# Threshold attention and a gated feed-forward block on one core: a smaller first part of the first batch, and its first block of tokens in two units

## The chip, the core and the metric

The kernel runs on one core of a Trainium2 chip. A core has five engines that run side by side, each with its own instruction stream in program order: TensorE (PE, matrix products into PSUM), VectorE (DVE), ScalarE (ACT), GpSimd (POOL) and SyncE (SP, which here issues the loads). They wait for each other through semaphores. The metric is the device time of one execution in microseconds (us), the median of several runs.

## The reference

```python
scores = scale * np.matmul(q, k.transpose(0, 1, 3, 2))        # (8 batches, 8 heads, 576, 576), head size 64
thresh = np.max(scores, axis=-1, keepdims=True) - tau
scores = np.where(scores >= thresh, scores, -1000000000.0)
scores = scores - np.max(scores, axis=-1, keepdims=True)
attn = np.exp(scores)
attn = attn / (np.sum(attn, axis=-1, keepdims=True) + 1e-09)
y = np.matmul(attn, v)
x = y.transpose(0, 2, 1, 3).reshape(4608, 512)                # tokens x model width
g = x @ w_gate                                                # 512 -> 1536
out = g * (1.0 / (1.0 + np.exp(-g))) * (x @ w_val) @ w_out    # 1536 -> 512
```

The three weight matrices arrive as 64-bit floats and are turned into 32-bit ones on the chip. All matrix products are in 32 bits; PE runs each as two instructions.

## The kernel before, in words

**Attention.** Heads are taken in pairs, four pairs to a batch, 32 in all. A *step* is one query tile of one pair: tiles 0 to 3 have 128 queries, tile 4 has 64. In a step PE makes the scores (L254 to L264), DVE takes their maximum (L274, L284), ACT makes the exponentials (L290), DVE applies the threshold and sums (L294), takes the reciprocal (L302), and ACT or POOL scales the rows (L308, L306). A full tile's scores fill both score buffers, so the next step's scores wait for this step's L294.

**Batch 0 is different.** Its four pairs are run in two parts: first tiles 0, 1 and 2 of each pair (`early`, `TA = 3` tiles, 384 queries), then tiles 3 and 4 of each (`rest`). So the first 384 tokens are complete for all heads before the rest is begun. In batch 0 PE turns the probabilities (L338) and multiplies by v (L361) within the next two steps. From batch 1 on (`halved`) all five tiles of a pair run in a row, DVE turns the probabilities (L320), and the product with v is made once per pair (L389), in the second step of the next pair. `prepare` (L591) puts a pair's q and k through DVE transposes at the end of the last step but one of the pair before; in batch 0 the queries that the first part does not use are kept in a spare arena.

**The feed-forward block** works on chunks of 384 tokens (`TC`), as *units* (chunk, first token, end). Chunk 1 is in two units of 192, since batch 0 ends in its middle; the others are whole. A unit runs through 12 slices `f` of the hidden width: `gate` (L423: four matmuls, then ACT copies the result to a `gt` tile, L434) and `value` (L436: four matmuls, then DVE multiplies with `gt` into `ht`, L442). Every second `f` an entry goes on the list `unsig`; when it holds three (`SIG`), `sigmoids` (L449) turns all entries: ACT makes the sigmoid of `gt` in place, with a table load before it and another when the next exponential comes, and POOL multiplies it into `ht` (L452). Only then is a `gt` tile free: there are four (`gp`, L76), each for two slices. `output` (L458) then makes rows of 128 tokens, in pieces of three slices (L466).

**PSUM.** Gates, values, outputs, turned probabilities and attention products take turns in four buffers (`ps_f`, L80).

**Weights.** They come in 24 pieces. Per step `fetch_weights` issues loads into free places on SP, `split_weights` lets ACT take one piece apart (L155, L156), and `join_weights` rebuilds it: four operations on DVE (L168 to L174) and two on POOL (L176, L177). The last pieces use only two places, so their split comes straight after their load. `need` forces joins when a slice lacks its weights.

**The order.** It is written out by the loop at the end (L633 on). Per step: scores; attention product or turning of earlier tiles; `fetch_weights` and `split_weights`; threshold and sum; join; half a share of feed-forward work (`fill`); scaling; `sigmoids` if three entries wait; the other half share; then loads and `prepare`. The share comes from `pace` (L570): the units left are spread over the steps until the next units are due, at the lowest rate over all horizons. `cost` counts a unit: one for each matmul of 384 tokens, four for each output piece. Units become ready (`give`) when their tokens are complete: the first at the start of the second part of batch 0.

Of the kernel before, what the change touches and what calls it, by code (L numbers as in the profile page):

```python
# [18 lines left out]
def kernel(  # L19
# [26 lines left out]
    nc = tc.nc  # L46
    P = 128
    B, H, S, D = q.shape
# [13 lines left out]
    TC = 384  # L62
    NCHUNK = B * S // TC
    NPAIR = B * NP
    TA = TC // P
    SCALE = 1.0 / float(D) ** 0.5
    assert 2 * D == P and NCC == NP and D == 2 * G and S - SM == 2 * G and 2 * S % TC == 0

# [349 lines left out]

    unsig = []

    def gate(j, cs, f, hts, gts):  # L423
# [56 lines left out]
    ready = deque()  # L480
    waiting = deque()
    for j in range(NCHUNK):
        if j == 1:
            waiting.extend([(1, 0, S - TC), (1, S - TC, TC)])
        else:
            waiting.append((j, 0, TC))

    def rows_of(unit):
        j, lo, hi = unit
        return range(lo // P, hi // P)  # L490

    def cost(unit):
        return 2 * NF * HCOST * (unit[2] - unit[1]) / TC + len(rows_of(unit)) * NF / OF * OCOST

    def supply(done):

        got = []
        while waiting and waiting[0][0] * TC + waiting[0][2] <= done:
            got.append(waiting.popleft())
        return got  # L500
# [3 lines left out]
    def block():  # L504
        late = iter(())
        while True:
            if not ready:
                yield from late
                if not ready:
                    yield 0  # L510
                continue
            unit = ready.popleft()
            j, lo, hi = unit
            cs = slice(lo, hi)
            hts, gts = hidden.setdefault(j, {}), {}
            c = HCOST * (hi - lo) / TC
            for f in range(NF):
                if f == (EARLY if j else 0):
                    yield from late
                gate(j, cs, f, hts, gts)  # L520
                yield c
                value(j, cs, f, hts, gts)
                yield c
            late = output(j, rows_of(unit), hts)
# [25 lines left out]
    arenas = [ptp.tile([P, 2 * NT + 1, S], F32, name="p") for _ in range(2)]  # L550
    early = list(range(TA))
    rest = list(range(TA, NT + 1))
    flat = [x.rearrange("p n s -> p (n s)") for x in arenas]
# [7 lines left out]
    for n, seg in enumerate(segs):  # L561
        done = 0
        if n == NP - 1:
            done = TC
        elif n % NP == NP - 1:
            done = n // NP * S
        seg["gives"] = supply(done)
        gains.append((len(seg["tiles"]), sum(cost(u) for u in seg["gives"])))
# [16 lines left out]
    kept = {}  # L585
# [5 lines left out]
    def prepare(seg):  # L591

        i = seg["i"]
        if i in kept:
            seg.update(kept[i])
            return
        qr, kr = raws[i]
        kept[i] = None
        qT = qkp.tile([P, S], F32, name="qT")
        if i < NP:  # L600
            kT = arenas[0][:, 4 + i, :]
            rest = flat[0][:, i * (S - TC):(i + 1) * (S - TC)]
            nc.vector.transpose(out=kT, in_=kr)
            nc.vector.transpose(out=qT[:, 0:TC], in_=qr[:, 0:TC])
            nc.vector.transpose(out=rest, in_=qr[:, TC:S])
            kept[i] = {"kT": kT, "qT": rest, "q0": TC}
        else:
            kT = qkp.tile([P, S], F32, name="kT")
            nc.vector.transpose(out=kT, in_=kr)
            nc.vector.transpose(out=qT, in_=qr)  # L610
        seg.update(kT=kT, qT=qT, q0=0)
# [6 lines left out]

    fetch_qk(0)
    prepare(segs[0])  # L620
    fetch_weights(1)
    fetch_qk(1)
# [4 lines left out]
    for n, seg in enumerate(segs):  # L627
        if NP <= n < 2 * NP:
            seg["v"] = segs[seg["i"]]["v"]
        for x, t in enumerate(seg["tiles"]):  # L630
# [37 lines left out]
            if x == len(seg["tiles"]) - 2 and n + 1 < len(segs):  # L668
                prepare(segs[n + 1])
                fetch_qk(segs[n + 1]["i"] + 1)  # L670
# [40 lines left out]
```

## Time and profile before

| | |
|---|---|
| median of 3 runs | 1619.55 us (1617.14 to 1622.19) |
| profiled execution | 1617.98 us, of which span 1616.2 us, mean granted PE clock 0.986 |
| busy PE, DVE, POOL, ACT | 1547.4, 1082.5, 771.3, 583.5 us |
| gate and value matmuls of 384 tokens | 1056 instructions each |
| gate and value matmuls of 192 tokens | 192 instructions each |
| first gate matmul | at 96.2 us |
| step 20, the first of batch 1, its L294 | at 167.59 us |
| ACT table loads | 23 before sigmoids, 22 before exponentials, 1.283 us each |

The span runs from the first to the last instruction. Busy times of PE are modelled, and overlapping matmuls are counted once. In lines of the profile, L433 is a line of the kernel, `pg<-xT,wgv` says what is written from what, x8 is a count, and the bracket at the end of a row says how long the engine sat idle before it and what ended that. In a group's row, "37.6, 340" are the busy time in us and the mean of one instruction in ns.

### The profile page before, as it was taken

The numbers are of one execution on the slowest core, as the hardware profiler recorded it, in microseconds if no ns is written. First come the engines' busy times: TensorE is split into PE (matmuls) and PEld (weight loads), VectorE is DVE, ScalarE is ACT, GpSimd is POOL, SyncE is SP. The second block draws the span as 40 slices with busy tenths as digits, with TensorE's granted clock in tenths as the row PEclk, the third lists the DMA queues.
The fourth block names the chain that finished last, engine by engine and source line by source line (L and its number), as shares of the span: only waits on it lengthen the run. The fifth ranks groups of instructions, "written<-read, shape, count | busy, mean of one in ns | idle before, by whom it ended". The sixth has DMA issues, their size and how long they took to land.

```text
span 1616.2 us, 27669 instructions
## 1 busy us (share of the span) xinstructions
PE 1547.4 (96%) x10192; PEld 831.2 (51%) x10192; DVE 1082.5 (67%) x3660; ACT 583.5 (36%) x1302; POOL 771.3 (48%) x686
## 2 busy tenths in 40 slices
PE   6899779899999999999999999999999999999998
PEld 4555444557545455455545545455545545455453
DVE  6977978876888778777766768677767767501000
ACT  6867543333324323323323424323323424312011
POOL 3545365555555645646545555645445554402011
PEclk9999889999999999999999999999999999999999
DMA  6542221111111111111011111111011110000000
GB/s 166 152 138 63 66 50 37 44 37 31 30 43 31 46 35 30 44 37 28 6 43 36 30 50 30 44 37 19 12 44 37 30 50 16 8 13 1 13 7 19
DMA packets 176343, 66.68 MB, mean 41 GB/s; under 512 B 159568, under 2 KB 159568, under 8 KB 176208
## 3 DMA queue, kind: packets, MB, share of 16 engines
q1 hardware_dynamic: 173328, 55.47, 15.1%
q0 software_dynamic: 2880, 9.44, 1.5%
q8 instruction: 81, 1.33, 0.3%
q14 instruction: 54, 0.44, 0.1%
HBM read 55.44 MB, written 9.44 MB: 40 GB/s over the span
## 4 chain that ended last, share of the span: by engine, by line
PE 77%; DVE 13%; ACT 4%; issue 3%; POOL 1%; DMA 1%; SPq 1%; DVEq 0%; POOLq 0%; ACTq 0%
PE pg L433 20%; PE pv L441 20%; PE po L466 19%; PE sc L254 8%; PE xa L389 8%; DVE p L294 3%; DVE mx L274 2%; DVE p L320 1%; ACT p L290 1%; DVE mx L231 1%; POOL p L306 1%; ACT L290 1%; SPq L203 1%; DVE sums L231 1%; POOL ht L452 0%
## 5 line engine op out<-in xcount | busy, mean ns | idle before, releaser
L306 POOL TENSOR_SCALAR p<-p,ri 128x288 f32<-128x288 f32 x486 | 479.0, 1001 | 439.2 <-DVE ri L302 435.1
L433 PE MATMUL pg<-xT,wgv 128*128 128x384 f32 (+1 forms) x1248 | 405.8, 469 | 6.0 <-ACT gt L434 4.0
L441 PE MATMUL pv<-xT,wgv 128*128 128x384 f32 (+1 forms) x1248 | 406.3, 469 | 0.0
L466 PE MATMUL po<-wo,ht 128*128 128x512 f32 x864 | 386.4, 599 | 1.2 <-POOL ht L452 1.2
L433 PEld LDWEIGHTS pg<-xT,wgv 128*128 128x128 f32 x1248 | 230.0, 191 | 159.2 <-issue 21.9
L441 PEld LDWEIGHTS pv<-xT,wgv 128*128 128x128 f32 x1248 | 231.5, 192 | 152.7 <-issue 17.8
L294 DVE SCALAR_TENSOR_TENSOR p<-sc,th,p 128x288 f32<-128x288 f32 (+1 forms) x540 | 258.3, 529 | 49.8 <-ACT p L290 48.6
L466 PEld LDWEIGHTS po<-wo,ht 128*128 128x128 f32 x864 | 160.1, 190 | 206.5 <-issue 194.6
L286 ACT ACTIVATE th<-nm,cut 128x4 f32<-128x4 f32 (+1 forms) x140 | 41.6, 297 | 554.3 <-DVE nm L277 554.3
L274 DVE TENSOR_REDUCE mx<-sc 128x2 f32<-128x576 f32 x252 | 179.5, 749 | 91.8 <-PE sc L254 91.6
L290 ACT ACTIVATE p<-sc,nm 128x288 f32<-128x288 f32 (+1 forms) x540 | 236.5, 510 | 0.6
L254 PE MATMUL sc<-kT,qT 64*32 64x288 f32 x4032 | 173.2, 416 | 29.9 <-DVE p L294 28.9
L442 DVE TENSOR_TENSOR ht<-gt,pv 128x384 f32<-128x384 f32 (+1 forms) x156 | 78.3, 510 | 177.5 <-PE pv L441 172.3
L320 DVE STREAM_TRANSPOSE p<-p 128x576 f32<-128x576 f32 x252 | 181.3, 754 | 0.8 <-POOL p L306 0.8
L452 POOL TENSOR_TENSOR ht<-ht,gt 128x768 f32<-128x768 f32 (+1 forms) x78 | 129.5, 1688 | 95.0 <-ACT gt L451 92.4
L254 PEld LDWEIGHTS sc<-kT,qT 64*32 64x32 f32 x4032 | 67.1, 107 | 139.2 <-issue 104.8
L434 ACT COPY gt<-pg 128x384 f32<-128x384 f32 (+1 forms) x156 | 70.7, 458 | 186.4 <-PE pg L433 182.3
L389 PE MATMUL xa<-p,vall 64*64 64x288 f32 x2016 | 132.1, 409 | 2.2 <-ACT gt L434 2.1
L389 PEld LDWEIGHTS xa<-p,vall 64*64 64x64 f32 x2016 | 77.3, 134 | 59.4 <-issue 15.1
L231 DVE TENSOR_REDUCE sums<-sums 32x4 f32<-32x4 f32 (+1 forms) x560 | 83.9, 150 | 10.5
L231 DVE TENSOR_REDUCE mx<-mx 32x4 f32<-32x4 f32 (+1 forms) x560 | 83.1, 148 | 10.5
L404 DVE COPY xT<-xa 128x96 f32<-128x96 f32 (+1 forms) x56 | 14.5, 296 | 111.4 <-PE xa L389 111.3
(73 smaller groups left out, 900.9 us busy)
## 6 DMA issues: line engine op xcount, KB each, us to landing
vall<-in_v_dram SPq DMA_DIRECT2D x112, 144.0 KB, 3.2
qraw<-in_q_dram SPq DMA_DIRECT2D x128, 72.0 KB, 2.3
kraw<-in_k_dram SPq DMA_DIRECT2D x128, 72.0 KB, 2.7
out_dram<-ob POOLq DMA_DIRECT2D x36, 256.0 KB, 2.4
wo<-in_moe_w_gate_dram SPq DMA_DIRECT2D x16, 384.0 KB, 3.4
wo<-in_moe_w_val_dram SPq DMA_DIRECT2D x16, 384.0 KB, 4.0
xT<-in_moe_w_out_dram SPq DMA_DIRECT2D x6, 768.0 KB, 5.7
wo<-in_moe_w_out_dram SPq DMA_DIRECT2D x2, 768.0 KB, 4.3
```

The source lines that it names most:

```text
L231: nc.vector.tensor_reduce(out=x[g * G:(g + 1) * G, 0:m, 1], in_=x[o * G:(o + 1) * G, 0:m, 0:1], axis=AX.X, op=ALU.max)
L254: nc.tensor.matmul(ps[g * G:(g + 1) * G, u, 0:SH], qT[hs, col + a * G:col + (a + 1) * G], kT[hs, c * SH:(c + 1) * SH], start=True, stop=True)
L274: nc.vector.tensor_reduce(out=mx[:, 2 * x:2 * x + 2, 0], in_=tile_[:, :, 0:SH], axis=AX.X, op=ALU.max, negate=True)
L290: nc.scalar.activation(ps[x], scs[x], AF.Exp, bias=nm[:, x:x + 1])
L294: nc.vector.scalar_tensor_tensor(out=ps[x], in0=scs[x], scalar=th[:, x:x + 1], in1=ps[x], op0=ALU.is_ge, op1=ALU.mult, accum_out=sm[:, x, ...
L306: nc.gpsimd.tensor_scalar(out=ps[x], in0=ps[x], scalar1=ri[:, x:x + 1], scalar2=None, op0=ALU.mult)
L320: nc.vector.transpose(out=p, in_=p)
L389: nc.tensor.matmul(xa[a][h * D:(h + 1) * D, at:at + n * G].rearrange("d (i q) -> d i q", q=G), vr[rs, h, j, :], p[rs, lo:lo + n, j, :], st ...
L433: nc.tensor.matmul(ps[:, 0:n], wgv[:, 0, c, f * P:(f + 1) * P], x[:, c, cs], start=(c == 0), stop=(c == NCC - 1))
L441: nc.tensor.matmul(ps[:, 0:n], wgv[:, 1, c, f * P:(f + 1) * P], x[:, c, cs], start=(c == 0), stop=(c == NCC - 1))
L452: nc.gpsimd.tensor_tensor(out=ht, in0=ht, in1=gt, op=ALU.mult)
L466: nc.tensor.matmul(po, hts[f // 2][:, f % 2, i * P:(i + 1) * P], wo[:, f, :], start=(f == 0), stop=(f == NF - 1))
```

## The change

`TA` becomes 2 and `QA = 256`: the first part of batch 0 takes tiles 0 and 1 of each pair, the second part tiles 2, 3 and 4. Chunk 0 is made in two units, of its first 256 and its last 128 tokens. The first is ready after the first part (8 steps in place of 12), the second when batch 0 is complete, together with the first half of chunk 1. The output rows of chunk 0 are all made after its second unit. Both units use the same `ht` tiles, each takes its own `gt` tiles. The transposes of a pair's queries are cut at 256 in place of 384.

```diff
-    TA = TC // P
+    TA = 2
+    QA = TA * P
...
     for j in range(NCHUNK):
-        if j == 1:
+        if j == 0:
+            waiting.extend([(0, 0, QA), (0, QA, TC)])
+        elif j == 1:
             waiting.extend([(1, 0, S - TC), (1, S - TC, TC)])
...
     def rows_of(unit):
         j, lo, hi = unit
-        return range(lo // P, hi // P)
+        return range(lo // P if j else 0, hi // P if j or hi == TC else 0)
...
         if n == NP - 1:
-            done = TC
+            done = QA
...
-            rest = flat[0][:, i * (S - TC):(i + 1) * (S - TC)]
+            rest = flat[0][:, i * (S - QA):(i + 1) * (S - QA)]
             nc.vector.transpose(out=kT, in_=kr)
-            nc.vector.transpose(out=qT[:, 0:TC], in_=qr[:, 0:TC])
-            nc.vector.transpose(out=rest, in_=qr[:, TC:S])
-            kept[i] = {"kT": kT, "qT": rest, "q0": TC}
+            nc.vector.transpose(out=qT[:, 0:QA], in_=qr[:, 0:QA])
+            nc.vector.transpose(out=rest, in_=qr[:, QA:S])
+            kept[i] = {"kT": kT, "qT": rest, "q0": QA}
```

## The prediction

> **What bounds the kernel now.** I read the page first, then busy time by stage (0 to 96 us: early part; 96 to 168: rest of batch 0; 168 to 264: batch 1 up to its second head pair; then the rest):
>
> ```profile
> PE 1547.4 (96%) x10192; PEld 831.2 (51%) x10192; DVE 1082.5 (67%) x3660; ACT 583.5 (36%) x1302; POOL 771.3 (48%) x686
> 0.00:96.00 96.00, 72.00 (x486) 47.55 (x488) 77.27 (x169) 72.88 (x137) 45.94 (x31) 0.95 0.60 155
> 96.00:168.00 72.00, 69.97 (x432) 41.06 (x431) 52.68 (x107) 45.03 (x82) 36.42 (x20) 0.98 0.31 92
> 168.00:264.00 96.00, 76.51 (x545) 41.80 (x545) 82.91 (x262) 42.44 (x95) 48.14 (x35) 0.89 0.23 55
> 264.00:1616.00 1352.00, 1328.88 (x8733) 700.82 (x8731) 869.63 (x3124) 423.17 (x991) 640.85 (x600) 1.00 0.13 29
> ```
>
> The first number after the stretch is its length, then PE, PEld, DVE, ACT, POOL. From 264 us on PE is busy 98%. So whatever the first 264 us lose or gain reaches the end, if the work left at that point is the same. PE idles 24 us in the first stage and 19 us in the third, where DVE is the busiest engine.
>
> I number the steps (one query tile of one pair) from 0 and take the first L294 of each as its clock. Before: step 7 at 58.82, 12 at 96.53, 20 at 167.59, 22 at 187.90, 24 at 208.28, 25 at 219.98, 26 at 231.50, 30 at 263.51.
>
> **The planner.** I worked its pace sums out for both versions. Cost unit: one 384-token matmul, 0.67 us (eight instructions, i.e. four matmuls, start 2.68 us apart). Before, it gives 6.9 units a step from step 12 on. After, 4.5 units from step 8 to 20, then 7.1. At step 20 both have 152 units to go (88+64 against 8+144), at step 30 both have 84, and later steps get the same fills but for one gate or value moved between neighbours. So the change is decided in steps 0 to 29.
>
> **What the skill says.** (1) TensorE: Matmul & The Clock Gate, "LDWEIGHTS (loading the stationary operand)": P/1.2 ns for P columns, 107 ns for 128. The trace agrees: four loads of 128 columns take 0.42 us. (2) ScalarE: Activation LUTs, "What ACT_TABLE_LOAD costs": 1283 ns and a drain of 1380 ns. The trace shows 1283 ns, with the sigmoid starting at once after it, so I use 1.28. (3) Perfetto Trace Analysis, "Tensor Engine Instruction (MATMUL, LD_WEIGHTS)": ACT, DVE and GPSIMD are strict FIFO. The trace agrees, below. (4) TensorE, "What's actually happening": an idle window of some 3.4 us halves the PE clock. After 5.32 us of idle at 188.97 the 32 score matmuls took 3.04 us, else 1.20.
>
> **The gain, steps 0 to 19.** An early step takes 6.5 us and is DVE's (its chain: p L294, weight join L168 to L174, maximum L284), while PE needs 4.5 us of it. Four such steps move behind the point where filler exists. The head transposes only move (they come at the end of steps 0, 2, 4). Step 8 now starts where step 11 less three would: 58.82 (step 7) + 1.0 (the first transposes wait for k, whose DMAs are issued until 13.04) + 6.5 + 3.4 (the wait for xa that step 12 shows at 92.9) = 69.7. The pair loads now come every two steps; SP is held by nothing longer than now, and the next load is issued 13 us before its use, against some 4 us to land.
> Steps 8 to 19: a full tile needs on PE 4.5 + a gate and a value of 256 tokens at 1.73 = 7.9 us, on DVE 7.0 (1.65+0.38 softmax, 2.74 join, 0.45 product, 1.42 maximum, 0.25 copy, gaps). A half tile is 6.3 on PE; a step with one gate only is DVE's 7.0. Adding step by step, whichever is larger: 84 us, plus 1.8 and 1.5 for the sigmoids that fall in step 15 (two table loads, and a join slowed by POOL's products, which step 19 shows: L168 1.55 for 0.54, L170 1.94 for 0.56), plus 1.4 for the transposes of step 18 and 1.8 for the dearer w_out joins: 90. Step 20 comes at 160.0 instead of 167.6: **-7.6 us**.
>
> **The loss, steps 20 to 29.** The second unit has 24 gates and values of 128 tokens. On PE they cost 0.90 us each (a third of 2.68; the weight loads, 0.105 each, just fit), no more in sum than before. But three to six of them come per step, and they share four PSUM buffers and the four gt buffers, and a gt is free only when POOL has multiplied it (L452). One place of the trace shows this ring closing, in the chain, in ACT's and in DVE's order of time:
>
> ```profile
> 385.45 3.94 POOL p L306 x4
> 389.39 0.97 POOL ht L452
> 390.38 0.33 ACT gt L434
> 390.75 2.85 PE pg L433 x8
> 390.38 0.32 ACT L434 COPY gt<-pg 128x192 f32<-128x192 f32 x1 [4.05 <-POOL ht L452]
> 390.73 0.35 DVE L442 TENSOR_TENSOR ht<-gt,pv 128x192 f32<-128x192 f32 x1 [5.22 <-ACT gt L434]
> ```
>
> Four sigmoids were queued in mid-step, and the next gate took the gt whose product stood behind the softmax scaling on POOL. ACT waits, DVE's product waits for ACT, the next maximum stands behind it on DVE: that step took 13.5 us (382.37 to 395.84) where one without takes 6.5.
> By the planner's order the change meets this twice: SIG of four entries falls in steps 22 and 25, followed at once by gate f=2 and gate f=10 of the new unit, which take the seventh and the eleventh gt, four after ones in that same SIG list. POOL's order there:
>
> ```profile
> 194.21 1.80 POOL L176 TENSOR_TENSOR lo<-lo,xT 128x768 f32<-128x768 f32 x1 [6.41 <-issue]
> 196.09 1.82 POOL L177 TENSOR_TENSOR wo<-wo,lo 128x768 f32<-128x768 f32 x1
> ...
> 226.40 1.81 POOL L176 TENSOR_TENSOR lo<-lo,xT 128x768 f32<-128x768 f32 x1 [8.67 <-DVE xT L174]
> 228.29 1.81 POOL L177 TENSOR_TENSOR wo<-wo,lo 128x768 f32<-128x768 f32 x1
> 230.09 3.93 POOL L306 TENSOR_SCALAR p<-p,ri 128x288 f32<-128x288 f32 x4
> ```
>
> - Step 22: join's last POOL operation ends 10.0 us after the step's start (197.9-187.9), then the product, 1.3 (between 1.00 at 384 and 1.81 at 768 elements), then gt 0.3, ht 0.3: DVE's next maximum starts at 11.9 instead of 6.1, and its exp meets a table load (nm to p 2.5 us for 1.35): +6.9.
> - Step 25: join until 10.1, L306 until 14.0 (step 25 is the first where POOL scales), product 0.7, gt and ht 0.5: the maximum starts at 15.3 instead of 6.7: +8.6. Its table loads are there before as well.
> - Step 24: five allocations. The fifth gate needs the PSUM that waits for ACT, and ACT stands in the split of the last weight piece until its DMA lands (216.06; now 7.94 us of idle that costs 2). The scores follow behind the fifth gate: +3.3, +0.5 for a cold PE.
> - Step 23: six allocations, the last value waits for the first one's product: +1.2. Step 26: fills of 5.7 us for 3.9 ahead of the attention product: +1.5. Steps 27 to 29: +1.4 (one more pair of table loads in 28, half hidden by the transposes; one output piece moved into 29).
>
> Together +23.4. Beyond: step 36 loses its pair of table loads (-1.1), step 39 gets a SIG of one and a value (+1.0).
> **Sum:** -7.6 + 23.4 - 0.1 = +15.7. Span 1616.2 to 1631.9, its run 1618.0 to 1633.7; the median before is 1.6 above that run, so 1635.
>
> **Unknown costs.** The 128-token matmul isn't in the FFN before: 0.90 us for eight at least; at most 1.48 (transposes of 128 columns: four in 0.59 with their gap). The difference, 192 x 0.07 = 13 us, lies in steps where PE idles 3 to 9 us, so 0 to 5 of it counts; I take 0. Products of 256 elements on POOL: 0.7, or 1.0 at most (as 384); one stands in the wait: 0 to 0.3. The join slowed by POOL: nothing to 2.9 (step 19's excess) per SIG; I take 1.5 in step 15 alone. Steps 8 to 19 with PE, DVE and ACT all near full: 84 is a floor without slips; 4 us worse is possible, and 3 better if DVE's gaps close.
>
> **Rivals.**
> 1. One stall of the two bites, or half of each (POOL done sooner because the joins come earlier within the step): +4 to +10, 1624 to 1630. For: the joins depend on ACT's split, which moves. Against: POOL's order is fixed in the program.
> 2. The two POOL waits don't occur (a gt comes free sooner), the PSUM ones do: -7.6 + 23.4 - 6.9 - 8.6 = +0.3, so 1615 to 1624. For: equal PE work. Against: the order above.
> 3. Faster: the small units hide whole. PE idles 19 us in the third stage and steps 20 to 24 are DVE's; if every gt and PSUM buffer is free when DVE ends its join (6.1 us into a step), steps 20 to 29 keep their 96 us and the early gain counts in full: 1612, 1608 to 1614. It decides at that 6.1 us. Against: the join alone holds POOL to 10.0.
> 4. Worse, 1643 to 1652: as forecast, and the 128-token matmuls at the upper price, PE at half clock in steps 22 to 26.
>
> **Chances.** Forecast 0.62 (1628 to 1642), rival 1 0.16, rival 2 0.09, rival 3 0.06, rival 4 0.07. The measurement can't tell differences under 0.3% (4.9 us). Faster: rival 3, 0.06. Within: most of rival 2 and a little of rival 1, 0.11. Slower 0.83. The range 1620 to 1645 leaves out rival 3, half of rivals 2 and 4.
>
> **What would show it.** First pg at about 70 us (now 96.2); step 20 at 160, step 30 at 279 (now 263.5). ACT's gt idle on POOL ht L452 about 3 us in step 22 and 7 in step 25; DVE's ht idle on gt 5 and 8 us. PE idle in the third stage up by 20 us or more, equal after. PE's sum up by little. The prediction is wrong if step 30 comes within 5 us of 263.5, or if the two versions part after it.

## The result and the profile after

The changed kernel takes 1632.28 us (1630.93 to 1634.52) against 1619.39 us (1617.14 to 1622.19) for the kernel before: 1.008 of its time, with an interval of 1.006 to 1.01. It is slower by about 13 us, where 15.7 were forecast. The profiled execution took 1632.9 us with a span of 1631.0; that is 14.8 us of span more than before.

Busy time of the engines of the changed kernel by stage, cut where its own steps 8, 20 and 30 begin (columns as before: the stretch, its length, busy PE, PEld, DVE, ACT, POOL, granted clock, DMA):

```profile
0.00:70.00 70.00, 52.32 (x324) 34.53 (x324) 51.59 (x117) 49.29 (x93) 31.52 (x23) 0.90 0.69 167
70.00:160.00 90.00, 88.21 (x650) 63.08 (x648) 76.01 (x161) 67.09 (x128) 48.58 (x28) 1.00 0.35 109
160.00:279.00 119.00, 82.28 (x679) 59.55 (x679) 83.75 (x268) 51.09 (x116) 52.96 (x44) 0.84 0.18 45
279.00:1631.00 1352.00, 1329.02 (x8735) 703.69 (x8733) 870.37 (x3127) 419.83 (x989) 638.96 (x598) 1.00 0.13 29
```

Batch 0 ends sooner, and PE is busy through nearly all of its second part. The third stage is 119 us long where it was 96, with almost the same DVE time in it (83.8 against 82.9 us): nearly all of the addition is waiting of DVE, whose work sets the pace there. From step 30 on the two kernels take 1352 and 1353 us.

| first L294 of step (L295 after) | before | forecast | after |
|---|---|---|---|
| 8 | 66.73 | 69.7 | 70.77 |
| 20 | 167.59 | 160.0 | 160.27 |
| 30 | 263.51 | 279 | 279.16 |
| length of step 22 | 9.64 | +6.9 | 16.61 (+6.97) |
| length of step 23 | 10.74 | +1.2 | 10.91 (+0.17) |
| length of step 24 | 11.70 | +3.8 | 17.63 (+5.93) |
| length of step 25 | 11.52 | +8.6 | 20.05 (+8.53) |
| length of step 26 | 12.07 | +1.5 | 12.30 (+0.23) |
| steps 20 to 29 together | 95.92 | +23.4 | 118.89 (+22.97) |
| steps 30 to 45 together | 132.33 | -0.1 | 130.43 (-1.90) |

The chain that ended last, in the stretch of steps 22 to 25 of the changed kernel (start, length, what; "issue" rows and short rows between the pieces are left out; its line numbers are one or two higher than in the kernel before: L436 is the gate's copy, L454 POOL's product, L307 the scaling):

```profile
186.61 1.82 POOL lo L177
188.51 1.80 POOL wo L178
190.31 1.23 POOL ht L454
191.56 0.28 ACT gt L436
191.86 0.29 DVE ht L444
192.15 1.34 DVE mx L275 x2
...
209.76 5.95 DMA xT<-in_moe_w_out_dram
216.54 0.88 ACT lo L157
217.62 2.08 PE pg L435 x8
219.70 2.21 PE sc L255 x32
221.91 1.41 DVE mx L275 x2
...
235.52 3.92 POOL p L307 x4
239.44 0.70 POOL ht L454
240.46 0.29 DVE ht L444
```

Its first and third piece are the forecast ring: the join's two POOL operations, in step 25 the scaling too, then the product that frees a `gt`, then the copy on ACT, then the product on DVE, and only behind that the next maximum. The second piece is step 24: a weight piece lands at 215.7, ACT takes it apart, then the fifth small gate gets its PSUM, and the scores of step 25 stand behind it on PE. ACT's own order of time gives the two waits:

```profile
191.56 0.27 ACT L436 COPY gt<-pg 128x128 f32<-128x128 f32 x1 [3.25 <-POOL ht L454]
...
240.16 0.27 ACT L436 COPY gt<-pg 128x128 f32<-128x128 f32 x1 [7.63 <-POOL ht L454]
```

3 and 7 us were forecast for them. They are what the experiments take apart.

### The profile page after: what moved, and what is told of

It is laid out like the page before. It is cut to its first block, busy times and chain, and to the rows that moved or that the text cites. A ratio compares the mean times of both kernels' runs of the same rounds, so it can differ in the third digit from the quotient of the medians.

```text
span 1631.0 us, 28105 instructions
## 1 busy us (share of the span) xinstructions
PE 1551.8 (95%) x10384; PEld 860.8 (53%) x10384; DVE 1081.7 (66%) x3672; ACT 587.3 (36%) x1322; POOL 772.0 (47%) x692
## 4 chain that ended last, share of the span: by engine, by line
PE 79%; DVE 11%; ACT 3%; issue 3%; POOL 2%; DMA 1%; SPq 1%; POOLq 0%; DVEq 0%; ACTq 0%
PE pg L435 20%; PE pv L443 20%; PE po L468 20%; PE sc L255 9%; PE xa L390 8%; DVE p L295 3%; DVE mx L275 2%; ACT p L291 1%; POOL p L307 1%; DVE p L321 1%; PE sc L260 1%; DVE mx L232 1%; ACT L291 1%; POOL ht L454 1%; PE tp L339 1%
## 5 line engine op out<-in xcount | busy, mean ns | idle before, releaser
L307 POOL TENSOR_SCALAR p<-p,ri 128x288 f32<-128x288 f32 x486 | 479.1, 1001 | 453.4 <-DVE ri L303 449.3
L435 PE MATMUL pg<-xT,wgv 128*128 128x384 f32 (+3 forms) x1344 | 415.1, 454 | 33.1 <-ACT gt L436 27.6
L443 PE MATMUL pv<-xT,wgv 128*128 128x384 f32 (+3 forms) x1344 | 410.1, 449 | 4.8 <-ACT gt L436 3.3
L435 PEld LDWEIGHTS pg<-xT,wgv 128*128 128x128 f32 x1344 | 247.1, 196 | 180.7 <-ACT gt L436 29.6
L443 PEld LDWEIGHTS pv<-xT,wgv 128*128 128x128 f32 x1344 | 245.8, 195 | 146.5 <-issue 12.5
L295 DVE SCALAR_TENSOR_TENSOR p<-sc,th,p 128x288 f32<-128x288 f32 (+1 forms) x540 | 258.3, 530 | 50.1 <-ACT p L291 49.5
L444 DVE TENSOR_TENSOR ht<-gt,pv 128x384 f32<-128x384 f32 (+3 forms) x168 | 80.0, 486 | 194.0 <-PE pv L443 170.1
L255 PE MATMUL sc<-kT,qT 64*32 64x288 f32 x4032 | 169.8, 416 | 13.9 <-DVE p L295 13.9
L454 POOL TENSOR_TENSOR ht<-ht,gt 128x768 f32<-128x768 f32 (+3 forms) x84 | 130.2, 1579 | 95.0 <-ACT gt L453 92.4
L436 ACT COPY gt<-pg 128x384 f32<-128x384 f32 (+3 forms) x168 | 72.7, 438 | 193.9 <-PE pg L435 178.9
L232 DVE TENSOR_REDUCE sums<-sums 32x4 f32<-32x4 f32 (+1 forms) x560 | 83.8, 150 | 10.5
```

The lines of the kernel that those rows point to most:

```text
L232: nc.vector.tensor_reduce(out=x[g * G:(g + 1) * G, 0:m, 1], in_=x[o * G:(o + 1) * G, 0:m, 0:1], axis=AX.X, op=ALU.max)
L255: nc.tensor.matmul(ps[g * G:(g + 1) * G, u, 0:SH], qT[hs, col + a * G:col + (a + 1) * G], kT[hs, c * SH:(c + 1) * SH], start=True, stop=True)
L295: nc.vector.scalar_tensor_tensor(out=ps[x], in0=scs[x], scalar=th[:, x:x + 1], in1=ps[x], op0=ALU.is_ge, op1=ALU.mult, accum_out=sm[:, x, ...
L307: nc.gpsimd.tensor_scalar(out=ps[x], in0=ps[x], scalar1=ri[:, x:x + 1], scalar2=None, op0=ALU.mult)
L435: nc.tensor.matmul(ps[:, 0:n], wgv[:, 0, c, f * P:(f + 1) * P], x[:, c, cs], start=(c == 0), stop=(c == NCC - 1))
L443: nc.tensor.matmul(ps[:, 0:n], wgv[:, 1, c, f * P:(f + 1) * P], x[:, c, cs], start=(c == 0), stop=(c == NCC - 1))
```

## The experiments

Theory: the early start is worth 7 us, and three waits, in steps 22, 24 and 25, lose some 21, because the 128-token unit hands its pieces out faster than the four `gt` buffers, the PSUM buffers and the in-order queues of ACT and POOL can turn them round. Rivals: small units cost by themselves (more pieces, more table loads); or the order of the tiles in batch 0 does it. Times of the kernel before beside these runs were 1620.26, 1619.91 and 1619.66 us.

### A fifth gt buffer, in the changed kernel and in the one before

```diff
-    gp = ctx.enter_context(tc.tile_pool(name="gp", bufs=4))
+    gp = ctx.enter_context(tc.tile_pool(name="gp", bufs=5))
```

> The changed kernel with five gt buffers in place of four. Ring theory (a gate in steps 22 and 25 waits for a gt whose product stands behind the join and the scaling on POOL): the two waits of ACT on POOL ht (3.25 and 7.63 us) vanish, and so does the one of 4.05 in step 45, which the kernel before has too. Step 22 takes 13.4 us in place of 16.6, step 25 takes 12.5 in place of 20.0, the time is 1617 to 1621. Rival (the small units cost by themselves: more pieces, more table loads): only step 45 gains, 1627 to 1630.

> Control: the kernel before with five gt buffers. Ring theory: it has one closing, in step 45 (ACT waits 4.05 us, DVE 5.22), so it gains 3 to 5 us: 1614 to 1616, and steps 0 to 30 stay within 0.3 us. Rival (the ring does not bind in the kernel before): 1619.

The changed kernel fell from 1632.28 to 1614.72 us (0.9961 of the kernel before, 0.9947 to 0.9976). Step 22 took 13.23 us, step 25 12.32, step 45 9.31. ACT's order of time in the changed kernel with five buffers:

```profile
186.53 1.98 ACT L453 ACTIVATE gt<-gt 128x512 f32<-128x512 f32 x4
188.42 0.24 ACT L436 COPY gt<-pg 128x128 f32<-128x128 f32 x1
...
228.69 0.42 ACT L453 ACTIVATE gt<-gt 128x256 f32<-128x256 f32 x1 [3.55 <-DVE ht L444]
229.01 0.25 ACT L436 COPY gt<-pg 128x128 f32<-128x128 f32 x1
```

Both copies now follow straight on the last sigmoid. Those two waits on POOL are gone (one of 1.5 us is left, in step 26), and with them 3.4 us of step 22 and 7.7 of step 25. The kernel before gained too, to 1616.03 us (0.9977, 0.9965 to 0.9989): the starts of its steps 0 to 25 lie within 0.3 us of those shown of the kernel before, and step 45 took 9.31 us for 13.47, the one place where its ring closed. (Its step 26 came out 1.7 us shorter as well, but not through the buffer: after the same wait of 2.1 us its attention products ran at a granted clock of 1.00 in place of 0.73.) Of the changed kernel's 17.6 us, 4.2 are that same step 45. The gain is larger than the 1617 to 1621 us that were expected, because steps 36 and 46 took 11.27 and 12.35 us for 12.93 and 13.71. In both, PE had run at a granted clock of 0.50 for some 3 us in the changed kernel and stayed at 1.00 here. For step 36 that is not the buffer's doing: with four buffers and the edit of step 25 shown below it took 11.26. The rival (small units by themselves) expected no gain outside step 45 and falls as the main cause. But two things are not cured by the buffer: step 24 stays at 17.36 us, and step 22 at 3.6 us above the kernel before.

### The split of chunk 0 alone

```diff
-        if j == 1:
+        if j == 0:
+            waiting.extend([(0, 0, 2 * P), (0, 2 * P, TC)])
+        elif j == 1:
...
-        return range(lo // P, hi // P)
+        return range(lo // P if j else 0, hi // P if j or hi == TC else 0)
```

> The kernel before with its first part of 384 queries, but chunk 0 in units of 256 and 128 tokens, both ready at step 12. By the planner's order no gate takes a gt from a sigmoid list of its own step, except in step 45. Ring theory: the split alone costs little: two more table loads, five allocations in step 24 and more small pieces in steps 21 to 25, +1 to +6: 1620 to 1626. Rival (small units cost by themselves): +13 to +20, 1632 to 1640, since all of the loss is there and none of the early gain.

1626.08 us (1.0032, 1.002 to 1.0043): +5.8, at the top of what the ring theory expected and under half of the rival's. Step 20 even came 1.7 us sooner. Where it goes is shown by the waits (of an execution that took 1628.27 us, 2.2 above the median). ACT's order of time, in steps 23 and 24:

```profile
205.40 1.28 ACT L451 ACT_TABLE_LOAD   x1
206.70 1.03 ACT L451 ACTIVATE gt<-gt 128x256 f32<-128x256 f32 x3
...
221.34 0.92 ACT L155 ACTIVATE wo<-xT 128x768 f32<-128x768 f32 x1 [7.78 <-DMA xT<-in_moe_w_out_dram]
```

PE's order of time, for the small values of steps 23 and 24:

```profile
203.72 1.37 PE L441 MATMUL pv<-xT,wgv 128*128 128x128 f32 x8 [3.20 <-ACT gt L434]
...
219.23 2.08 PE L441 MATMUL pv<-xT,wgv 128*128 128x128 f32 x8 [5.24 <-DVE ht L442]
```

Steps 21, 23 and 24 took 12.97, 14.08 and 14.42 us for 10.21, 10.74 and 11.70. In steps 21 and 23 a small gate's copy stands on ACT behind a table load and three sigmoids, in step 23 also behind a weight piece that landed at 201.83; DVE's product and the next maximum stand behind the copy. In step 24 it is the landing of the last weight piece that holds ACT, and it took 7.1 us from its issue where it took 6.0 in the changed kernel. No gate waited for POOL's product there. So small units do have a price of their own, some 6 us, and in this kernel it is a price of waits in queues, the added table loads among them; the matmuls themselves start 0.89 us apart for eight, a third of the 2.68 for 384 tokens.

### The first part alone

Chunk 0 stays one unit, so that nothing of it is ready before batch 0 is complete:

```diff
-            waiting.extend([(0, 0, QA), (0, QA, TC)])
+            waiting.append((0, 0, TC))
```

> The other part of the change alone: the first part has 256 queries, but chunk 0 stays one unit of 384 tokens, so it is ready only when batch 0 is complete. There are no small gates and no filler before step 21; 208 units wait at step 21 in place of 149. Theory (what the early part gives is PE work under DVE's steps): step 20 comes at 140 to 150, but 56 units (37 us) more are left there, of which idle PE of steps 20 to 40 takes up about half: 1620 to 1634. Rival (the order of the tiles matters by itself, not the filler): 1612 or less.

1626.97 us (1.0043, 1.0029 to 1.0057). Step 20 came at 152.30, a little later than expected, with 56 units more to go there. In the first 152 us PE is busy 117 us, at a mean granted clock of 0.85 (0.96 in the kernel before up to its step 20); its busy time over the whole span is 8 us above that of the kernel before. So with four buffers neither part of the change is a gain alone, and the early start is worth something only through the filler that it lets in.

### The last weight piece ahead of the next pair's loads

In step 23 `prepare` is followed by the loads of the next q and k, which wait on SP for the transposes and then take 4.6 us to issue. The last weight piece of step 24 stands behind them. Here the pair's loads go after it, in that step alone:

```diff
-                fetch_qk(segs[n + 1]["i"] + 1)
+                if n == 2 * NP:
+                    owed = segs[n + 1]["i"] + 1
+                else:
+                    fetch_qk(segs[n + 1]["i"] + 1)
...
                 fetch_weights(2)
+                if n == 2 * NP and x == NT:
+                    fetch_qk(owed)
```

> The changed kernel, where in step 23 the loads of the next pair's q and k are moved on SP behind the last weight piece's load of step 24. Theory for step 24 (ACT stands in the split until that piece lands, and through PSUM the scores stand behind it): the piece is issued at 205 in place of 209.8 and lands 4.4 us sooner, step 24 takes 13.2 us in place of 17.6, the time is 1627 to 1629. Rival (the fifth small gate costs by itself, whatever lands when): step 24 stays at 17 to 18 us, 1632.

1625.83 us, and step 24 fell from 17.63 to 11.03. SP's order of time:

```profile
204.74 0.39 SPq L145 DMA_DIRECT2D xT<-in_moe_w_out_dram  x1
205.17 2.93 SPq L204 DMA_DIRECT2D qraw<-in_q_dram  x4
```

The piece is issued 5.0 us sooner and lands at 209.28 in place of 215.74. Without the eight loads ahead of it it also took 4.5 us in place of 6.0 from issue to landing, which is why the gain is 6.6 us where 4.4 were expected. (In all runs of this case it took 5.7 to 7.9 us behind those loads, seven times, and 4.5 to 4.6 ahead of them, four times.) The rival (the fifth small gate by itself) is refuted: the gate is still there. The wait for POOL in steps 22 and 25 stayed, at 3.25 and 7.64 us, so the two causes are separate.

### Who stands before the product on POOL

In step 25 alone the rows are scaled on ACT:

```diff
-            if halved and not split:
+            if halved and not split and not (seg["i"] == NP + 1 and t == 0):
```

> The changed kernel, where ACT in place of POOL scales the rows in step 25 alone. Theory (the gt of step 25 stands behind the join, 3.6 us, and the scaling, 3.94 us, on POOL): the product starts 3.9 us sooner, step 25 takes 16.1 in place of 20.05 us, the time is 1628 to 1629. Rival (ACT's table loads and sigmoids set the end of step 25): no gain, or a loss of up to 2 us for ACT's added 1.8.

1628.98 us (1.0056, 1.0042 to 1.0071), and step 25 took 16.12 us where 16.1 was expected. POOL's order of time:

```profile
232.90 1.82 POOL L177 TENSOR_TENSOR lo<-lo,xT 128x768 f32<-128x768 f32 x1 [16.27 <-DVE xT L175]
234.80 1.80 POOL L178 TENSOR_TENSOR wo<-wo,lo 128x768 f32<-128x768 f32 x1
236.56 2.77 POOL L454 TENSOR_TENSOR ht<-ht,gt 128x256 f32<-128x256 f32 x4
```

The product now follows on the join. The 3.94 us of scaling came off the step whole, though ACT had 1.8 us more to do: POOL's queue set the end of that step. (Step 24 was 2.0 us longer in this execution than in the changed kernel. The edit does not reach it: the last weight piece took 7.93 us from issue to landing in place of 5.95. Why the landing took longer is open.)

### Both cures together, with and without the change

The edits of the fifth buffer and of the weights first, in both kernels:

> The changed kernel with five gt buffers and with the pair's loads of step 23 behind the last weight piece. If the two causes are separate, the gains add: step 22 13.2 us, step 24 11, step 25 12.3 to 12.5, step 45 9.3, and 1614.7 becomes 1607 to 1610, clearly below the kernel before with five gt buffers (1616.0). Rival (the same waiting seen from two sides): no better than 1613.

> Control: the same two edits in the kernel before. There the last piece's late landing costs DVE the 2.1 us of step 25's first wait, since only two gates and values stand in step 24: 1616.0 becomes 1613 to 1615, step 24 takes 9.6 in place of 11.7 us. With the run of both edits in the changed kernel it gives what the change is worth without its waits: 4 to 8 us faster. Rival (the early start is lost in any case): the two are equal within 2 us.

The changed kernel took 1610.78 us (0.9943, 0.9931 to 0.9955), the one before 1613.35 us (0.9956, 0.9943 to 0.9968). The gains did not quite add (1608.3 would be the sum, and 1607 to 1610 were expected), and the change is worth 2.6 us on this footing, where 4 to 8 were expected; the two intervals overlap a little. Part of what is missing is the clock: steps 35 and 36 took 7.61 and 11.87 us for 6.64 and 11.27 with the fifth buffer alone, with PE at 0.50 for some 3 us there. The steps show where the rest went: the lead of 7.2 us at step 20 (160.35 against 167.55) is a lag of 1.1 at step 30, since step 22 takes 13.24 us for 9.63, step 24 11.56 for 9.27, step 25 12.31 for 11.48 and step 28 8.54 for 7.24. Steps 30 to 45 then return 3.8.

### What was left in step 22

In step 22 alone the sigmoids are issued after the second half of the filler:

```diff
+            later = n == 2 * NP and x == 2
-            if len(unsig) >= SIG:
+            if len(unsig) >= SIG and not later:
                 sigmoids()
             fill(part)
+            if later:
+                sigmoids()
```

> The changed kernel with both edits (five gt buffers, weights first), and in step 22 alone the four sigmoids are issued after the second half of the filler in place of before it. Theory for what is left in step 22 (13.24 us, 9.6 in the kernel before): ACT copies the gate behind the table load and the sigmoids, and DVE's product and the next maximum stand behind that copy. Then step 22 takes 11.4 to 11.9 us and the time goes from 1610.8 to about 1609. Rival (the three small products and the last value's wait for PSUM make it): 13 us, no gain.

1607.39 us (0.9922 of the kernel before, 0.9909 to 0.9935), and step 22 took 11.53. ACT's order of time:

```profile
184.66 0.24 ACT L436 COPY gt<-pg 128x128 f32<-128x128 f32 x1
184.92 1.28 ACT L453 ACT_TABLE_LOAD   x1
186.22 1.98 ACT L453 ACTIVATE gt<-gt 128x512 f32<-128x512 f32 x4
```

The copy stands ahead of the table load. Half of step 22's rest was ACT's queue, as expected. Step 24 gained 1.2 us as well, which nobody had forecast. There the fifth gate ran at a granted clock of 1.00 and took 1.16 us, after PE had been idle for 3.88; with two edits it took 2.08 at 0.50, after 3.60. Whether the third edit brings that about or it is the chance of one execution isn't shown. This version is the fastest of all that were run, 12.3 us below the kernel before, and 6.0 us below that kernel with the two edits that apply to it too (1613.35 us; the intervals lie apart). The third edit is for sigmoids that the kernel before doesn't have in step 22: its table loads fall in steps 18 and 25. The first part of 256 queries does pay once its three waits are shortened; edits made for the kernel before alone were not looked for.

## Why the prediction was right, and where its terms were off

**The planner.** That everything is decided in steps 0 to 29 held nearly: the difference in span is -7.32 (steps 0 to 19), +22.97 (20 to 29), -1.90 (30 to 45) and +1.05 after, together +14.8. The third term was put at -0.1, as -1.1 in step 36 and +1.0 in step 39. Those came at +1.27 and +0.09: step 36 did lose its table loads, but PE ran at a granted clock of 0.50 ahead of its attention product (at 1.00, in the run with a fifth buffer, it took 11.27 us, 0.4 less than in the kernel before). What made the -1.90 is above all step 31. The planner shifts one output piece out of step 31, where PE sets the pace because of the attention product, and that step took 9.17 us for 11.16. A piece that moves between neighbouring steps isn't free when only one of the two has PE to spare.

**The gain.** Step 8 was forecast at 69.7 and came at 70.77; step 20 at 160.0 and came at 160.27. The sum of whichever engine is larger, step by step, held to within a microsecond in all: steps 8 to 19 took 89.5 us. (The terms given for them add up to 90.5, not 90.) Single terms were right by luck. Step 15 took 10.40 us, some 3.6 more than steps 9 and 12, where 3.3 were charged for sigmoids; but 1.5 of these were for a join slowed by POOL, and its join ran at its usual pace (0.54 and 0.56 us for L169 and L171). DVE waited 3.91 us for ACT instead, where both table loads and the sigmoids stood ahead of the exponentials. The slowed join itself was misread: in the kernel before, step 19's join is of a w_out piece, whose L168 and L170 otherwise take 0.66 and 0.69, so its excess was about 2.3 us and not 2.9. The first gate started at 70.44.

**The ring.** Steps 22 and 25 came at +6.97 and +8.53 for +6.9 and +8.6, with DVE's waits at 4.99 and 8.38 us for 5 and 8. The working rested on one place of the profile before, step 45, and on POOL's strict order. The fifth buffer removed both waits, and the scaling on ACT removed its own 3.9 us from one. This is shown, not only argued.

**Step 24** was mis-sized: +5.93 for +3.8. The mechanism was right (the moved load cured it), the term for a cold PE was not: 0.5 was taken. PE's order of time:

```profile
217.62 2.08 PE L435 MATMUL pg<-xT,wgv 128*128 128x128 f32 x8 [9.07 <-ACT gt L436]
219.62 2.17 PE L255 MATMUL sc<-kT,qT 64*32 64x288 f32 x32
```

Warm, such rows are 1.06 and 1.20 us long, so the cold PE cost about 2 us, and the first maximum waited for all of the scores. The remaining half microsecond of the miss isn't taken apart. The Trainium skill's half clock after an idle window (TensorE: Matmul & The Clock Gate, "What's actually happening") fits both durations, and the granted clock in the trace is 0.50 over both rows; it should have been charged in full where a wait leaves PE idle ahead of scores that DVE is waiting for.

**Steps 23 and 26** were charged 1.2 and 1.5 and cost 0.17 and 0.23. In step 23 the last value was assumed to wait for the first one's product; PE's order of time shows otherwise:

```profile
199.42 2.08 PE L435 MATMUL pg<-xT,wgv 128*128 128x128 f32 x8 [4.03 <-ACT gt L436]
201.29 1.91 PE L443 MATMUL pv<-xT,wgv 128*128 128x128 f32 x8
```

The last gate waited for a copy on ACT, and the value followed on it without a wait. DVE's first product of the step came only at 203.03, behind the join. The buffer of a gate comes free with ACT's copy, so the wait for PSUM is not simply "four allocations back". In step 26 the charge was right and luck covered it. The attention product, before and after:

```profile
232.51 6.27 PE L389 MATMUL xa<-p,vall 64*64 64x288 f32 x68 [2.09 <-ACT gt L434]
...
247.96 5.06 PE L390 MATMUL xa<-p,vall 64*64 64x288 f32 x72
```

It got going 1.01 us into the step before (but for four of its matmuls) and 2.46 after, 1.45 later, as charged. But it ran at a mean granted clock of 0.73 before and 1.00 after, which gave 1.2 us back. PE's idle time in the stage rose from 19 to 37 us (119 less 82.3, against 96 less 76.5), 17 more where 20 had been named as a sign. The two errors together (-2.3) nearly cancel the one of step 24 (+2.1): the sum was better than its terms.

**The rivals.** Rival 3 (small units hide whole) falls: they cost 5.8 us alone. Rivals 1 and 2 (one wait, or none) fall by the two waits in the trace. Rival 4's dearer 128-token matmul did not show: warm pieces of eight start 0.89 us apart. Its half clock did show, at 0.50 in parts of steps 22 to 25; what that cost in step 24 is given above, and no run separates its cost in the other steps. What the prediction did not say is that the loss was curable by one buffer and one reordered load, and that the change would then gain.

## What to carry to other kernels

When filler work is cut into smaller pieces, count per step how many buffers of each pool it takes and which operation frees each one, and follow that operation back on its own engine's queue: here four buffers closed a ring through PE, ACT, POOL and DVE. One existing stall of the same kind in the profile before (13.5 us for one step) priced the new ones within 0.1 us. A step's length in one profiled execution can be off by 1 to 2 us through the clock alone, as steps 26 and 36 show, so a small gain is better read from the waits than from one step. And before judging a reordering by its time, give it the buffer it needs: the same change went from 0.8% slower to 0.8% faster with three small edits around it, two of which gave the kernel without the change 0.4%.

## What the runs showed of the hardware

The price of a piece of eight matmul instructions is nearly proportional to its tokens down to 128: starts 2.58 to 2.68 us apart at 384 tokens, 1.30 at 192, 0.89 at 128, all with warm PE. At a granted clock of 0.50 the row of a piece of 128 is 2.08 us long, where warm ones are 1.06. How long a wait turns the clock down is not one number here (the prediction took some 3.4 us): it stood at 0.50 right after 3.10 us of idle in the changed kernel (at 191.88) and still at 1.00 after 3.88 in the run with three edits, and after the same 2.1 us it went down in step 26 of the kernel before and did not in that kernel with a fifth buffer. The landing of one 768 KB weight piece took 5.7 to 7.9 us behind the eight loads of q and k, and 4.5 to 4.6 us ahead of them.
